# A global-filter FFT block with a SwiGLU feed-forward on one core: the transforms one unit later, output stores in four places, the first filter piece after the rows, turned rows kept by lanes

## The chip, the core and the metric

The kernel runs on one core of a Trainium2 chip. The core has a matrix engine (TensorE, "PE" in the profile, with its weight loads as "PEld"), VectorE ("DVE"), ScalarE ("ACT"), GpSimd ("POOL") and SyncE ("SP", which here only issues transfers). Each engine works through its own instructions in their order; engines wait for one another by semaphores. Sixteen DMA engines carry the transfers. The metric is the device time of one execution in microseconds (us), the median of several runs.

## What is computed

The input is x, 8 batches of 3008 tokens with 256 channels. Along the tokens a real FFT is taken, multiplied by a complex filter, and transformed back. Every one of the 24,064 resulting rows then goes through a gated feed-forward with 1536 hidden units. All in 32-bit floats.

```python
def _attn_ref(x, filt_r, filt_i):
    X = np.fft.rfft(x, axis=1)
    F = (filt_r + 1j * filt_i)[None, :, :]
    y = np.fft.irfft(X * F, n=x.shape[1], axis=1)
    return y.astype(np.float32)

def _moe_ref(x, w_gate, w_val, w_out):
    g = x @ w_gate
    silu = g * (1.0 / (1.0 + np.exp(-g)))
    val = x @ w_val
    return (silu * val @ w_out).astype(np.float32)
```

## The kernel before

**Units.** The rows after the transform lie in `y_t`, channels on partitions, and are worked on in 47 stripes of 512 rows. A stripe has 12 units, one for each 128 hidden units; there are 564 units, and the loop at the end of the kernel runs over them. Its turn n holds the gate and value products of unit n (`products`, L925 and L929, results ws and wx), their evaluation on ScalarE and VectorE (L247, L952, L951, L954, result h), the split of h of unit n-1 into two parts of fewer bits and their sum (`split_high`, `split_low`: hh, hl, hs; the latter two on GpSimd, L241), and the product of unit n-2 with the output weights (`project`, L979 to L982, two halves c). The first 24 units (stripes 0 and 1) are "plain": they use whole-precision weights (L915, L974) while the split weights are still being made. After the last unit of a stripe the sums are taken out of the accumulators (`evacuate`: turn n with n % 12 == 1, two ScalarE and two VectorE instructions), transposed on VectorE in the next turn (`turn_out`, L1001), and stored in the one after (`store`, four quarters q, one transfer each, or more pieces in batch 0).

**Places in a turn.** A turn has places for other work, "a", "b", "c", "p" and "z": "a" at its start, "b" between gate and value, "c" before the projections, "p" between the two halves of the projection. Work for a place is entered with `at(n, place, f)` or, for a generator that runs up to its next `yield` at each place, with `steps`. This fixes the order on each engine's queue.

**Weights.** Six of the twelve weight pieces stay on the chip, six are fetched anew for each stripe, always two units ahead in that list: at "a" of every other turn SP issues a piece of the gate and value weights (gv, 768 KB) and one of the output weights (wo, 384 KB), L1064. Each waits for the last product that read its place.

**Transforms.** 3008 is 47 x 64. Batch 0 is transformed ahead of the loop. For each later batch b, the transform is spread over the turns while earlier rows go through the feed-forward, counted from u0 = 60 + 72 (b - 2), or 0 for b = 1. Its steps:
- `turn_rows` (four parts, at u0 - 24, -22, -20, -18; for b = 1 all at turn 0) copies rows of x in reverse order, from DRAM to a DRAM buffer `turned`; `load_x(g)` reads a group of them and the straight rows into `lent`, `fold(g)` makes sums and differences on VectorE (four instructions, two in each of two turns).
- `quads(g)`, g = 0 to 3: two bursts of products (L619), copies and sums (the VectorE copy is L636, the last sums are on GpSimd), four stores to `quads_dram`. After g = 3, `load_four(0)` reads them back, turned round.
- `there(w)`, w = 0 to 5: a burst (L713), then the product with the filter (`load_filter(w)`, 1 MB) on VectorE and GpSimd, for which one half is exchanged by an SBUF to SBUF transfer (lent<-raw); its last sum is on VectorE (L238).
- `home(w)`, five turns after there(w): a burst (L688), a copy on ScalarE, two sums on VectorE, two stores to `d2`.
- `load_t4(k)` and `back(k, m)`: eight bursts (L772), each with two transposes on VectorE into `y_t` (L778).

The numbers `q_at`, `there_at`, `home_at`, `back_at`, `first_fold` are the turns of these steps. For b > 1 quads begin at u0 + 1, 5, 9, 13, there at 20, 26, ... 50, home at 25, ... 55, back at 60, 61, 63 to 68. `split_y` splits the next stripe of `y_t` into parts, at places listed in `free`, `later` and `after`. The buffer `lent` is shared by all of it (`room_of`); its x rows, the filter piece and t4 lie in the same place. Products rotate over four accumulator banks; a burst takes the two that come next.

**SP's queue.** All of these transfers, the weights' and the output's too, are issued by SP in the order in which the places come. If one has to wait, those behind it wait too. Only weight loads of the first stage go by GpSimd's queue.

Of the kernel before, what the change touches and what calls it, by code (L numbers as in the profile page):

```python
# [129 lines left out]
def kernel(  # L130
# [62 lines left out]

    dram_tiles = [wdpool.tile([2 * NS, N2, C], FP32, name=f"d2_{i}") for i in range(2)]
    quads_dram = [wdpool.tile([64, N2, C], FP32, name=f"quads_{i}") for i in range(2)]
    turned_dram = [wdpool.tile([16, 128, C], FP32, name=f"turned_{i}") for i in range(2)]
    gv_dram = wdpool.tile([ND, 128, 2, 2, 3, 128], F32R, name="gv_all")
    wo_dram = wdpool.tile([ND, 128, 2, 3, 128], F32R, name="wo_all")
    f_dram = wdpool.tile([128, 2, NS, C], FP32, name="filter")
# [221 lines left out]
    class Spectral:  # L421
# [146 lines left out]
        def turn_rows(self, part):  # L568

            xb, to = x[self.b], self.turned  # L570
            end = NS if self.b > 2 else 32
            h, lane, n = part // 2, 32 * part, 16 * part
            p = 1 - h
            self.load(out=to[:, lane + p:lane + end],
                      in_=bass.AP(tensor=xb.tensor, ap=[[C, 16], [-N2 * C, end - p], [1, C]],
                                  offset=xb.offset + ((N1 - 1) * N2 + n) * C))
            if h == 0:
                self.load(out=to[:, lane], in_=xb[n:n + 16])

        def load_x(self, u):  # L580
            if u < N_QUAD // 2:
                self.x[u] = [room_of("x", n) for n in range(2)]
                up, down = self.x[u]
                at = self.turned.rearrange("(g q) p c -> g p q c", q=4)[u]
                self.load(out=down.rearrange("p (q c) -> p q c", c=C), in_=at)
                rows = x[self.b].rearrange("(r n) c -> r n c", n=N2)
                for n in range(4):
                    first = 16 * n + 4 * u
                    self.load(out=up[ts(n, 32)].rearrange("p (q c) -> p q c", c=C),
                              in_=rows[0:32, first:first + 4])  # L590
# [14 lines left out]
        def quads(self, g):  # L605

            pieces = (g, g + N_QUAD // 2)
            parts = self.x.pop(g)
            t1 = {u: room_of("yg"[i]).rearrange("p (n h c) -> p n h c", h=2, c=C)
                  for i, u in enumerate(pieces)}  # L610
            views = {}

            def burst(h):
                banks = {u: bank(f"qa_{self.b}_{u}_{h}") for u in pieces}
                for cp in range(2):
                    for t in range(2):
                        for i, u in enumerate(pieces):
                            r, c = 32 * (2 * h + i), 32 * (2 * cp + t)
                            pin(nc.tensor.matmul(  # L619
                                out=banks[u][c:c + 32], lhsT=quad_t[r:r + NS, ts(t, 32)],  # L620
                                rhs=parts[t][r:r + NS, ts(cp, NV * C)],
                                start=True, stop=True))
                for u, t in banks.items():
                    views[u, h] = t.rearrange("p (n c) -> p n c", c=C)

            d1 = self.quads_dram.rearrange("a (n h) c -> a n (h c)", h=2)
            v, e, act = nc.vector, nc.gpsimd, nc.scalar
            a, b = pieces
            burst(0)
            if g == 3:  # L630
                self.load_filter(0)
                self.load_turns(0)
            yield
            pin(act.copy(out=t1[a][:, :, 0], in_=views[a, 0]))
            yield
            pin(v.tensor_copy(out=t1[b][:, :, 0], in_=views[b, 0]))  # L636
            yield
            burst(1)
            yield
            m = t1pool.tile([128, 2 * NV, C], FP32, name=f"raw_{self.b}_{g}", tag="t1", bufs=1)[:, 0:NV]  # L640
            pin(act.copy(out=m, in_=views[b, 1]))
            yield
            pin(sub(v, t1[a][:, :, 1], t1[a][:, :, 0], views[a, 1]))
            pin(add(v, t1[a][:, :, 0], t1[a][:, :, 0], views[a, 1]))
            yield
            pin(sub(e, t1[b][:, :, 1], t1[b][:, :, 0], m))
            yield
            pin(add(e, t1[b][:, :, 0], t1[b][:, :, 0], m))
            yield
            for u in pieces:  # L650
                for cp in range(2):
                    n = 4 * u + 2 * cp
                    self.load(out=d1[:, n:n + 2], in_=t1[u][64 * cp:64 * cp + 64])
            if g == 3:
                self.load_four(0)

        def load_four(self, w):

# [344 lines left out]
    def store(u):  # L1003
        o, j = evacuated[u.j].rearrange("p i z c -> p i (z c)"), u.j

        def rows(q, t0, t1, i0, i1, token, step):
            pin(nc.sync.dma_start(
                out=bass.AP(tensor=out.tensor, offset=out.offset + token * C + 64 * q,
                            ap=[[step * C, t1 - t0], [32 * step * C, i1 - i0], [1, 64]]),
                in_=o[32 * q + t0:32 * q + t1, i0:i1]))  # L1010

        end = min(max(S - T * j, 0), T)
        pieces = []
        for k in range(NCHUNK):
            a, b = max(T * j, NK0 * k), min(T * j + end, NK0 * (k + 1))
            while a < b:
                i, t0 = divmod(a - T * j, 32)
                full = (b - a) // 32
                if t0 or not full:
                    n, t1 = 1, min(32, t0 + b - a)  # L1020
                else:
                    n, t1 = full, 32
                pieces.append((t0, t1, i, i + n, 4 * (a - NK0 * k) + k, 4))
                a += (t1 - t0) if n == 1 else 32 * n
        if end < T:
            pieces.append((0, 32, end // 32, 16, T * j + end, 1))
        for q in range(4):
            for piece in pieces:
                rows(q, *piece)


    units_of = []
# [12 lines left out]
    def at(n, place, f, *args):  # L1045
        hooks.setdefault((n, place), []).append((f, args))
# [6 lines left out]
    def lazily(make):  # L1053

        def piece():
            yield from make()

        return piece()
# [49 lines left out]
    for b in range(1, B):  # L1108
        s = specs[b]
        if b == 1:  # L1110
            u0, q_at, there_at = 0, [5, 8, 11, 14], [18, 22, 27, 32, 37, 42]
            home_at = [m + 4 for m in there_at]
            back_at, first_fold = range(51, 59), [(4, "a"), (4, "b"), (4, "c"), (5, "a")]
        else:
            u0 = 60 + BATCH * (b - 2)
            q_at, there_at = [1, 5, 9, 13], [20 + 6 * w for w in range(N_FOUR)]
            home_at = [m + 5 for m in there_at]
            back_at = (60, 61, 63, 64, 65, 66, 67, 68)
            first_fold = [(-1, "b"), (-1, "c"), (0, "a"), (0, "b")]
            for part in range(4):  # L1120
                at(u0 - 24 + 2 * part, "c", s.turn_rows, part)
            at(u0 - (3 if b == 2 else 7), "c" if b == 2 else "a", s.load_x, 0)
        at_u0 = lambda places: [(u0 + m, p) for m, p in places]
        fold = lambda g, s=s: lazily(lambda: s.fold(g))
        steps(fold(0), at_u0(first_fold))
# [14 lines left out]
        for k, n, place in ((1, home_at[-1] + 2, "c"), (0, home_at[-1] + 3, "b"), (2, home_at[-1] + 3, "c"),  # L1140
                            (3, back_at[1] + 1, "a")):
            at(u0 + n, place, s.load_t4, k)
        for n, (k, m) in zip(back_at, ((1, 0), (1, 1), (0, 0), (0, 1), (2, 0), (3, 0), (2, 1), (3, 1))):
            n += u0
            steps(lazily(lambda s=s, k=k, m=m: s.back(k, m)), [(n, "p"), (n + 1, "a"), (n + 1, "a")])

# [4 lines left out]
    for j in range(PLAIN, NSTRIPE):  # L1151
# [3 lines left out]
        m = (n - 60) % BATCH or BATCH  # L1155
        free = {24: "17b 17b 17c 18b 18c 18c 19b 19c", 36: "22b 22b 22c 23b 28b 28b 28c 31b",
                48: "36b 36b 36c 37b 40b 40b 41b 42b", 60: "48b 48b 48c 49b 50b 50b 50c 51b"}.get(n)
        later = {12: "0b 1b 1c 2b 3b 4b 5b 6b", 24: "15b 16b 17b 18b 17b 18b 19b 20b",
                 36: "24b 24b 25b 26b 28b 29b 31b 32b", 48: "36b 36b 37b 38b 40b 41b 43b 44b",
                 60: "48b 48b 49b 50b 52b 53b 55b 56b", 72: "60b 60b 60c 61b 62b 62b 62c 63b"}[m]  # L1160
        after = "67b 67b 67c 68b 68b 68b 69b 70b" if n > 60 else "57b 57b 57c 58b 58b 58b 58c 59b"

        def places_of(text, base):
# [25 lines left out]
    def projections(n, u):  # L1189
        if u:  # L1190
            u.project(0)
            if u.last:
                evacuate(u, 0)
        run_hooks(n, "p")
        if u:
            u.project(1)
            if u.last:
                evacuate(u, 1)
                end = n + 1 if n < NU else n
                for c in range(2):  # L1200
                    at(end, "c", turn_out, u, c)
                at(end + 1, "a", store, u)
        run_hooks(n, "z")

    for n in range(NU + 2):
# [23 lines left out]
        if n != N_PLAIN + 1:  # L1229
            projections(n, two_back)  # L1230
        if n == NU + 1:
            for m in (n, n + 1, n + 2):
                for place in "abcp":
                    run_hooks(m, place)
    assert not hooks, sorted(hooks)
# [28 lines left out]
```

## Time and profile before

| | |
|---|---|
| runs | 2769.06, 2769.44, 2774.63 us; median 2769.44 |
| profiled execution | 2778.99 us, of which 2777.2 are the span from the first to the last instruction |
| TensorE's granted clock | 0.994 of full speed on average |
| instructions | 44,446 |
| DMA | 598.16 MB, 215 GB/s, 311,118 packets |
| first non-plain product | 224 us |
| batches 2 to 7, six periods of 72 units | 399.5 to 2468.1 us: 349.1, 344.3, 342.5, 342.2, 343.0, 347.4 |
| after that, feed-forward alone | to the end |

A matrix product of 128 x 512 is shown with some 390 ns, but products overlap: in an undisturbed stretch one begins every 0.227 us. So a nearly always busy TensorE can still be slowed, and the time of a turn says more than the busy share. The groups of the page: line, engine, operation, result<-operands, form, count, then busy us and mean ns of one, then the idle time of the engine before them and what ended it.

```profile
L929 PE MATMUL wx<-yh,gv 128*128 128x512 f32 x2160 | 850.2, 394 | 23.4 <-DVE lent L238 11.5
L925 PE MATMUL ws<-ys,gv 128*128 128x512 f32 x2160 | 673.2, 393 | 24.4 <-DMA gv<-gv_all 15.8
L954 DVE TENSOR_TENSOR h<-wx,g 128x512 f32<-128x512 f32 x540 | 373.7, 692 | 72.3 <-DVE wx L247 2.4
L241 POOL TENSOR_TENSOR hs<-hh,hl 128x512 fp32r<-128x512 f32 x540 | 717.4, 1329 | 42.3
```

### The profile page before, as it was taken

Reading aid. Unit: us, or ns where it says so; the run is one execution under the profiler, and the core shown is the slowest. Engines: PE = TensorE matmul, PEld = TensorE weight load, DVE = VectorE, ACT = ScalarE, POOL = GpSimd, SP = SyncE. Lnnn points to the kernel's source line nnn. Section 1 sums busy time; section 2 is a strip of 40 time slices with the busy share of each in tenths; the row PEclk is TensorE's granted clock in tenths of the full one; section 3 lists DMA queues with packets and bytes.
Section 4 is the critical chain, followed back from the end, with each engine's and each line's share of the span. In section 5 each row is a group of like instructions: output and inputs, shape, how many; then the busy total and the mean of one; then the engine's idle time right before and its main releaser. Section 6 shows DMA issues by size and latency. Waiting matters only on the chain.

```text
span 2777.2 us, 44446 instructions
## 1 busy us (share of the span) xinstructions
PE 2698.5 (97%) x14476; PEld 2005.1 (72%) x14476; DVE 1844.4 (66%) x2600; ACT 1821.0 (66%) x3433; POOL 1980.0 (71%) x1613
## 2 busy tenths in 40 slices
PE   8999999999999999999999999999999999999998
PEld 6446776777767776677777777777777677778886
DVE  5885677566785667756677666776667756665554
ACT  5555665676666666677666666666666667666775
POOL 3675766787677776787767777677866777777775
PEclk9999999999999999999999999999999999999999
DMA  9967777778577785777857778577785777744443
GB/s 232 315 198 222 253 200 225 218 245 237 179 229 225 246 242 164 232 239 240 245 169 224 235 246 241 169 238 237 235 243 159 229 225 238 230 137 154 159 154 106
DMA packets 311118, 598.16 MB, mean 215 GB/s; under 512 B 124378, under 2 KB 181624, under 8 KB 310424
## 3 DMA queue, kind: packets, MB, share of 16 engines
q1 hardware_dynamic: 308136, 587.33, 69.0%
q0 software_dynamic: 2608, 7.93, 1.0%
q8 instruction: 116, 1.90, 0.3%
q14 instruction: 114, 0.93, 0.1%
q10 hardware_dynamic: 144, 0.07, 0.0%
HBM read 486.56 MB, written 104.60 MB: 213 GB/s over the span
## 4 chain that ended last, share of the span: by engine, by line
PE 72%; DMA 7%; DVE 7%; POOL 6%; ACT 3%; issue 3%; SPq 1%; DVEq 0%; POOLq 0%; ACTq 0%
PE wx L929 28%; PE ws L925 14%; PE o L979 8%; PE o L980 7%; PE o L982 7%; PE wpd L772 2%; POOL hs L241 2%; DMA gv<-gv_all 2%; POOL hl L241 2%; PE wqc L688 2%; DVE lent L241 1%; PE wqb L713 1%; DMA lent<-raw 1%; PE wqa L619 1%; DMA quads<-lent 1%
## 5 line engine op out<-in xcount | busy, mean ns | idle before, releaser
L241 POOL TENSOR_TENSOR hl<-h,hs 128x512 fp32r<-128x512 f32 x540 | 698.8, 1294 | 609.3 <-ACT hs L244 568.0
L929 PE MATMUL wx<-yh,gv 128*128 128x512 f32 x2160 | 850.2, 394 | 23.4 <-DVE lent L238 11.5
L929 PE MATMUL wx<-yl,gv 128*128 128x512 f32 x2160 | 843.5, 391 | 0.0
L241 POOL TENSOR_TENSOR hs<-hh,hl 128x512 fp32r<-128x512 f32 x540 | 717.4, 1329 | 42.3
L244 ACT ACTIVATE hh<-h 128x512 fp32r<-128x512 f32 x540 | 341.7, 633 | 551.8 <-DVE h L954 479.9
L925 PE MATMUL ws<-ys,gv 128*128 128x512 f32 x2160 | 673.2, 393 | 24.4 <-DMA gv<-gv_all 15.8
L247 DVE SCALAR_TENSOR_TENSOR g<-wx,g 128x512 f32<-128x512 f32 x540 | 372.2, 689 | 376.0 <-ACT g L244 304.6
L247 DVE SCALAR_TENSOR_TENSOR wx<-wx,v 128x512 f32<-128x512 f32 x540 | 377.2, 698 | 322.7 <-PE wx L929 185.7
L929 PEld LDWEIGHTS wx<-yh,gv 128*128 128x128 f32 x2160 | 406.7, 188 | 136.5 <-PE ws L925 26.5
L925 PEld LDWEIGHTS ws<-ys,gv 128*128 128x128 f32 x2160 | 405.1, 189 | 121.5 <-PE wx L929 15.2
L929 PEld LDWEIGHTS wx<-yl,gv 128*128 128x128 f32 x2160 | 406.7, 188 | 83.2
L979 PE MATMUL o<-hs,wo 128*128 128x512 f32 x1080 | 443.7, 411 | 8.3 <-POOL hs L241 8.1
L980 PE MATMUL o<-hh,wo 128*128 128x512 f32 x1080 | 422.7, 391 | 0.0
L982 PE MATMUL o<-hl,wo 128*128 128x512 f32 x1080 | 421.7, 390 | 0.0
L954 DVE TENSOR_TENSOR h<-wx,g 128x512 f32<-128x512 f32 x540 | 373.7, 692 | 72.3 <-DVE wx L247 2.4
L244 ACT ACTIVATE g<-ws 128x512 f32<-128x512 f32 x540 | 317.5, 588 | 71.8 <-PE ws L925 69.2
L952 ACT ACTIVATE g<-g 128x512 f32<-128x512 f32 x540 | 343.8, 637 | 12.6 <-DVE g L247 12.0
L951 ACT COPY v<-ws 128x512 f32<-128x512 f32 x540 | 314.7, 583 | 38.2 <-PE ws L925 34.9
L244 ACT ACTIVATE hs<-h 128x512 fp32r<-128x512 f32 x540 | 337.2, 624 | 0.0
L979 PEld LDWEIGHTS o<-hs,wo 128*128 128x128 f32 x1080 | 202.7, 188 | 145.8 <-issue 95.3
L982 PEld LDWEIGHTS o<-hl,wo 128*128 128x128 f32 x1080 | 203.2, 188 | 43.5
L980 PEld LDWEIGHTS o<-hh,wo 128*128 128x128 f32 x1080 | 203.4, 188 | 34.7
(113 smaller groups left out, 2415.4 us busy)
## 6 DMA issues: line engine op xcount, KB each, us to landing
gv<-gv_all SPq DMA_DIRECT2D x268, 768.0 KB
wo<-wo_all SPq DMA_DIRECT2D x268, 384.0 KB
lent<-filter SPq DMA_DIRECT2D x42, 1024.0 KB
quads<-lent SPq DMA_DIRECT2D x112, 256.0 KB
out_dram<-o SPq DMA_DIRECT2D x172, 128.0 KB
lent<-quads SPq DMA_DIRECT2D x168, 128.0 KB
lent<-raw SPq DMA_DIRECT2D x84, 256.0 KB
d<-lent SPq DMA_DIRECT2D x84, 256.0 KB
```

Of the source, the lines that this page charges most:

```text
L241: return eng.tensor_tensor(out=dst, in0=a, in1=b, op=ALU.subtract)
L244: return nc.scalar.activation(out=dst, in_=a, func=AF.Copy, scale=scale)
L247: return nc.vector.scalar_tensor_tensor(out=dst, in0=a, scalar=scale, in1=b, op0=ALU.mult, op1=op)
L688: pin(nc.tensor.matmul(out=home[e][s // 2 * 64:s // 2 * 64 + 64, s % 2 * C:s % 2 * C + C], lhsT=tb[r, 1, 64 * s:64 * s + 64], rhs=y[r, s], ...
L925: pin(nc.tensor.matmul(out=s, lhsT=w[:, a, 2], rhs=yb[:, a], start=a == 0, stop=a == 1, skip_group_check=True))
L929: pin(nc.tensor.matmul(out=p, lhsT=w[:, a, n], rhs=t[:, a], start=a + n == 0, stop=a + n == 2, skip_group_check=True))
L951: pin(nc.scalar.copy(out=v, in_=s))
L952: pin(nc.scalar.activation(out=self.g, in_=self.g, func=AF.Silu))
L954: pin(nc.vector.tensor_tensor(out=self.h, in0=p, in1=self.g, op=ALU.mult))
L979: pin(nc.tensor.matmul(out=s, lhsT=w[:, c, 2], rhs=both, stop=self.last, **kw))
L980: pin(nc.tensor.matmul(out=p, lhsT=w[:, c, 0], rhs=hi, stop=False, **kw))
L982: pin(nc.tensor.matmul(out=p, lhsT=w[:, c, 1], rhs=lo, stop=self.last, **kw))
```

## The change

- For batches 2 to 7 quads, there, home and back begin one unit later or up to two (back is now at 62 to 69 without a gap, in another order of its parts, also for batch 1), and the first fold with them; load_x(0) moves from u0 - 7 to u0 - 4 for batches 3 to 7. The places of `split_y` in `later` move too. `turn_rows` stays where it was.
- `store` yields after each quarter, so that the transfers of a stripe are issued at four places of two turns.
- `load_filter(0)` is issued after `load_four(0)` instead of at the first burst of quads(3).
- `turned` is laid out as [128 lanes, 16 rows, channels] instead of [16, 128, channels]. `load_x` reads 4 KB in one piece for each lane. `turn_rows` writes, as its outermost dimension, two groups of 8 rows, each 8 KB in one piece, for 23 to 32 lanes; before it wrote 16 rows, each 1 KB, for as many lanes.

```diff
--- before.py
+++ after.py
@@ -193,7 +193,7 @@
 
     dram_tiles = [wdpool.tile([2 * NS, N2, C], FP32, name=f"d2_{i}") for i in range(2)]
     quads_dram = [wdpool.tile([64, N2, C], FP32, name=f"quads_{i}") for i in range(2)]
-    turned_dram = [wdpool.tile([16, 128, C], FP32, name=f"turned_{i}") for i in range(2)]
+    turned_dram = [wdpool.tile([128, 16, C], FP32, name=f"turned_{i}") for i in range(2)]
     gv_dram = wdpool.tile([ND, 128, 2, 2, 3, 128], F32R, name="gv_all")
     wo_dram = wdpool.tile([ND, 128, 2, 3, 128], F32R, name="wo_all")
     f_dram = wdpool.tile([128, 2, NS, C], FP32, name="filter")
@@ -571,18 +571,17 @@
             end = NS if self.b > 2 else 32
             h, lane, n = part // 2, 32 * part, 16 * part
             p = 1 - h
-            self.load(out=to[:, lane + p:lane + end],
-                      in_=bass.AP(tensor=xb.tensor, ap=[[C, 16], [-N2 * C, end - p], [1, C]],
+            self.load(out=to[lane + p:lane + end].rearrange("p (a n) c -> a p (n c)", a=2),
+                      in_=bass.AP(tensor=xb.tensor, ap=[[8 * C, 2], [-N2 * C, end - p], [1, 8 * C]],
                                   offset=xb.offset + ((N1 - 1) * N2 + n) * C))
             if h == 0:
-                self.load(out=to[:, lane], in_=xb[n:n + 16])
+                self.load(out=to[lane], in_=xb[n:n + 16])
 
         def load_x(self, u):
             if u < N_QUAD // 2:
                 self.x[u] = [room_of("x", n) for n in range(2)]
                 up, down = self.x[u]
-                at = self.turned.rearrange("(g q) p c -> g p q c", q=4)[u]
-                self.load(out=down.rearrange("p (q c) -> p q c", c=C), in_=at)
+                self.load(out=down.rearrange("p (q c) -> p q c", c=C), in_=self.turned[:, ts(u, 4)])
                 rows = x[self.b].rearrange("(r n) c -> r n c", n=N2)
                 for n in range(4):
                     first = 16 * n + 4 * u
@@ -628,7 +627,6 @@
             a, b = pieces
             burst(0)
             if g == 3:
-                self.load_filter(0)
                 self.load_turns(0)
             yield
             pin(act.copy(out=t1[a][:, :, 0], in_=views[a, 0]))
@@ -653,6 +651,7 @@
                     self.load(out=d1[:, n:n + 2], in_=t1[u][64 * cp:64 * cp + 64])
             if g == 3:
                 self.load_four(0)
+                self.load_filter(0)
 
         def load_four(self, w):
 
@@ -1027,6 +1026,7 @@
         for q in range(4):
             for piece in pieces:
                 rows(q, *piece)
+            yield
 
 
     units_of = []
@@ -1113,13 +1113,13 @@
             back_at, first_fold = range(51, 59), [(4, "a"), (4, "b"), (4, "c"), (5, "a")]
         else:
             u0 = 60 + BATCH * (b - 2)
-            q_at, there_at = [1, 5, 9, 13], [20 + 6 * w for w in range(N_FOUR)]
+            q_at, there_at = [2, 6, 10, 14], [21 + 6 * w for w in range(N_FOUR)]
             home_at = [m + 5 for m in there_at]
-            back_at = (60, 61, 63, 64, 65, 66, 67, 68)
-            first_fold = [(-1, "b"), (-1, "c"), (0, "a"), (0, "b")]
+            back_at = range(62, 70)
+            first_fold = [(0, "b"), (0, "c"), (1, "a"), (1, "b")]
             for part in range(4):
                 at(u0 - 24 + 2 * part, "c", s.turn_rows, part)
-            at(u0 - (3 if b == 2 else 7), "c" if b == 2 else "a", s.load_x, 0)
+            at(u0 - (3 if b == 2 else 4), "c" if b == 2 else "a", s.load_x, 0)
         at_u0 = lambda places: [(u0 + m, p) for m, p in places]
         fold = lambda g, s=s: lazily(lambda: s.fold(g))
         steps(fold(0), at_u0(first_fold))
@@ -1140,7 +1140,7 @@
         for k, n, place in ((1, home_at[-1] + 2, "c"), (0, home_at[-1] + 3, "b"), (2, home_at[-1] + 3, "c"),
                             (3, back_at[1] + 1, "a")):
             at(u0 + n, place, s.load_t4, k)
-        for n, (k, m) in zip(back_at, ((1, 0), (1, 1), (0, 0), (0, 1), (2, 0), (3, 0), (2, 1), (3, 1))):
+        for n, (k, m) in zip(back_at, ((1, 0), (1, 1), (0, 0), (2, 0), (3, 0), (0, 1), (2, 1), (3, 1))):
             n += u0
             steps(lazily(lambda s=s, k=k, m=m: s.back(k, m)), [(n, "p"), (n + 1, "a"), (n + 1, "a")])
 
@@ -1155,9 +1155,9 @@
         m = (n - 60) % BATCH or BATCH
         free = {24: "17b 17b 17c 18b 18c 18c 19b 19c", 36: "22b 22b 22c 23b 28b 28b 28c 31b",
                 48: "36b 36b 36c 37b 40b 40b 41b 42b", 60: "48b 48b 48c 49b 50b 50b 50c 51b"}.get(n)
-        later = {12: "0b 1b 1c 2b 3b 4b 5b 6b", 24: "15b 16b 17b 18b 17b 18b 19b 20b",
-                 36: "24b 24b 25b 26b 28b 29b 31b 32b", 48: "36b 36b 37b 38b 40b 41b 43b 44b",
-                 60: "48b 48b 49b 50b 52b 53b 55b 56b", 72: "60b 60b 60c 61b 62b 62b 62c 63b"}[m]
+        later = {12: "0b 0b 1b 2b 4b 5b 6b 7b", 24: "12b 12b 14b 15b 16b 17b 18b 19b",
+                 36: "24b 24b 26b 27b 29b 30b 32b 33b", 48: "36b 36b 38b 39b 41b 42b 44b 45b",
+                 60: "48b 48b 50b 51b 53b 54b 56b 57b", 72: "60b 60b 60c 61b 62b 62b 62c 63b"}[m]
         after = "67b 67b 67c 68b 68b 68b 69b 70b" if n > 60 else "57b 57b 57c 58b 58b 58b 58c 59b"
 
         def places_of(text, base):
@@ -1199,7 +1199,7 @@
                 end = n + 1 if n < NU else n
                 for c in range(2):
                     at(end, "c", turn_out, u, c)
-                at(end + 1, "a", store, u)
+                steps(lazily(lambda: store(u)), [(end + 1, "a"), (end + 1, "c"), (end + 2, "a"), (end + 2, "c")])
         run_hooks(n, "z")
 
     for n in range(NU + 2):
@@ -1229,7 +1229,7 @@
         if n != N_PLAIN + 1:
             projections(n, two_back)
         if n == NU + 1:
-            for m in (n, n + 1, n + 2):
+            for m in range(n, n + 4):
                 for place in "abcp":
                     run_hooks(m, place)
     assert not hooks, sorted(hooks)
```

## The prediction

> **What bounds the kernel now.** I read the page first, then TensorE's waits, then its instructions in order of time, unit by unit, then SP's queue and the DMA records.
>
> ```profile
> PE 2698.5 (97%) x14476; PEld 2005.1 (72%) x14476; DVE 1844.4 (66%) x2600; ACT 1821.0 (66%) x3433; POOL 1980.0 (71%) x1613
> ```
>
> TensorE is never idle for long: 78.7 of 2777.2 us. Its waits, by what ended them:
>
> ```profile
> PE ws L925 <- DMA gv<-gv_all: 15.8, 6, 5.1
> PE wx L929 <- DVE lent L238: 11.5, 19, 0.6
> PE o L979 <- POOL hs L241: 8.1, 8, 2.3
> PE wx L929 <- DVE lent L636: 6.3, 10, 1.9
> ```
>
> (us in total, times, longest.) None is large; what they cost is read from slots. I call "slot n" the stretch from the first L925 product of unit n to that of unit n+1, and +m the slot u0+m of a batch. Undisturbed, a slot is 4.08 us (18 products, 0.227 us from one to the next); with a burst of there, home or back 5.33, with half a quads 5.5. The six periods of 72 slots of batches 2 to 7 take 2068.5 us. Undisturbed, one would take 72 x 4.08 for the products, 20 bursts x 1.25 and 8 halves of quads x 1.43: 330.5, six 1983. So 85 us at most can be won there, and every transfer that comes late can lose more.
>
> The DMA engines are the second resource:
>
> ```profile
> 284.00:332.00 48.00, 46.71 (x247) 35.34 (x246) 31.47 (x45) 34.58 (x65) 39.09 (x31) 1.00 0.86 289
> 635.00:671.00 36.00, 33.72 (x179) 25.48 (x177) 24.07 (x34) 25.02 (x47) 26.76 (x21) 1.00 0.80 255
> 2500.00:2550.00 50.00, 50.00 (x222) 41.40 (x221) 27.73 (x41) 35.16 (x66) 33.63 (x27) 1.00 0.47 162
> ```
>
> (Window; busy us of PE, PEld, DVE, ACT, POOL; granted clock, DMA share, GB/s.) In the stretches where the next batch's rows are turned, the sixteen are busy 80 to 86% of the time; beside the plain feed-forward of the end 47%.
>
> **The change, part by part.** Sums are made against the profiled execution (2778.99 us, span 2777.2), which is 9.5 over the median 2769.44; I put the difference on the median.
>
> *One slot later.* (1) At +20 TensorE waits for gv: slots +19 and +20 last 13.59, 14.00, 11.46, 11.60, 11.52 and 16.05 us in batches 2 to 7 instead of 4.08 + 5.33, in all 21.8 too long (with the half clock that follows three of the waits). SP issued that gv, due at slot 17 "a", only at +18, because the quads stores and `load_four(0)` at 16 "c" stand before it and wait for GpSimd's sum and for the stores' landing. One slot later they stand behind it, and the next gv has until +22: it follows 0.5 MB of quads rows (16 packets x 0.121 us per engine, 2.5 as they came here), 1 MB of filter (16 x 0.159) and 0.4 MB of wo (8 x 0.121), takes 8 x 0.234 itself, in all 8 us from the landing of the quads stores at about 19 + 1.6, and has 2 to 3 us to spare. I take -21.8 (bounds -21.8 and 0). (2) At +26, +38 and +50 home meets the stripe's evacuation: 6.20 instead of 5.33 us, 15.7 us in all. After, home meets the two transposes (L1001, 0.69 each), and the sum of `there` on VectorE (L238, 1.44) now stands ahead of the evacuation. VectorE's order becomes h(25), that sum, two evacuations (0.69 each), g(26), wx(26), h(26), two transposes, home's two sums. Laid out by these durations, g(26) ends at 3.8 in slot 26, where the burst wants its bank at 3.5: 0.35; home's second sum ends at 2.1 in slot 27, where the next wx wants its bank at 1.8: 0.45 with the semaphore. Together 0.80. I take -1 (bounds -15.7, +6). (3) back at +61 with the evacuation makes +62 1.38 too long; at +62 it meets the transposes instead, and my layout gives 0.97: -2.5 (bounds -8.3, 0). (4) New: fold(3) ends at 13 "c", in front of the evacuation. Its last half (1.5) and the two evacuations (1.37) precede g(14), whose bank the quads burst needs: slot +14 about 2.1 too long, where +13 to +15 were 1.2 before. +5 for six (bounds 0, +9). (5) raw leaves SP in an even slot, away from gv, wo and the output: up to -6 (slots +54, +55), but the rows below stand there, so 0. (6) The rest that moves: `load_x(0)` three slots later still has four slots (17 us; its 1 MB landed some 8 us after its issue at 1745); `load_t4(3)` at +64 lands within 6 us, as from 1726.9, and back(3,0) uses it at +66, 14 us on; the splits of y move with the transforms, with the same count of instructions on ScalarE and GpSimd: 0 (a late one costs what its wait lasts).
>
> *Stores one by one.* In batch 2 stripe 5 has sixteen pieces; they hold SP from 416.7 to 426.3, the quads store comes late, VectorE's L636 too, and +6 lasts 9.29 instead of 5.52: -3.8 (bounds -3.8, 0). Elsewhere the same issues stand in four places; nothing else waits for them.
>
> *Filter piece behind the rows.* 16 packets of 4 KB by 0.159 us per engine, first read at +22: hidden by there(0) and the slots +19 to +21, 0 (2.5 us a batch if the slack above is gone). It passes the four quads stores, `load_four(0)` and the wo and gv of slots 15 and 17, which now leave without it.
>
> *Turned rows by lanes.* Reading them changes from 32 packets of 1 KB (46 ns) per engine to 8 of 4 KB (159): -0.2 us each, hidden. Writing them is what I expect to decide. Before, such a store is [16] x [23 to 32] pieces of 1 KB: 23 x 46 ns = 1.07 us (1.46 for 31 or 32 rows), on all sixteen engines. After, it is [2] x [23 to 32] pieces of 8 KB. Do two rows spread over sixteen engines?
>
> ```profile
> wf_t<-wf_tbl SPq DMA_DIRECT2D x1, 47.0 KB
> turned<-in_x_dram SPq DMA_DIRECT2D x10, 384.0 KB
> turned<-in_x_dram SPq DMA_DIRECT2D x10, 368.0 KB
> ```
>
> The trace has a transfer that tells: wf_t is 94 rows of 512 B, and its packets start in pairs, 47 pairs, from 1.67 to 3.05 us, 27 ns each: two engines at work. The completion writes agree: a transfer on sixteen engines leaves sixteen packets of 4 bytes, 1697 transfers of SP would leave 27,152, and there are 27,034. With 2 engines for the 94 rows, 14 for each of eight transfers of 14 rows and 4 for each of six of 4 rows, 102 of the 118 missing are explained (16 are one transfer's). So the number of engines follows the outermost count, and for 2 rows I take two engines. The Trainium skill, "DMA: Bandwidth & Descriptors", section "Why a DMA increments its semaphore by 16 and not by 1", says the same: as many engines, up to 16, as divide the slowest dimension of both sides; by it the sum stands. Its "Specifications" put an engine at about 27 GiB/s, by which the 38.9 us below would be an estimated 36.
>
> The price of 8 KB on one engine: the fastest such packets of the trace took 0.309 us, and 24 KB from DRAM to DRAM 0.912, the same rate. So 7.1 to 7.4 us a store (23, 24 rows), 9.6 to 9.9 (31, 32), on two engines in whose queues all later transfers of SP have a share.
>
> Batch 1: four stores at once.
>
> ```profile
> 70.85 3.94 SPq L438 DMA_DIRECT2D turned<-in_x_dram  x6
> 82.45 0.37 SPq L438 DMA_DIRECT2D lent<-turned  x1
> 95.12 0.69 DVE L238 TENSOR_TENSOR lent<-lent 128x512 f32<-128x512 f32 x1
> ```
>
> Here SP waits 6.2 us for them, and fold(0) starts at 95.1. After: 126 packets x 0.309 = 38.9 us from about 73.5, and seven weight loads of GpSimd's queue share the engines (16 x 46 ns or 8 x 121, 0.85 each): 118. Then `load_x(0)`, 6.5 us as now: 125. fold(0) waits for it, every VectorE instruction behind it too (h of the plain units, the weights' rounding), and TensorE stops: +30 (bounds +20, +38).
>
> Batch 2 (rows stored at units 36 to 42, 284 to 332 us): an engine is busy 0.86 x 48 = 41.3 us, less 4 x 1.46 of the old stores 35.5, plus 39.0: 74.5 in 48. Batches 3 to 7 (slots +48 to +54): 0.80 x 36 = 28.8, less 4.3, plus 29.0: 53.5 in 36. Too much by 26.5 and 17.5; the last gv of the window has some 10 us to spare (issued 666.7, needed 680.1, 2.9 for itself and wo). So 16.5 once, and 7.5 five times; with the clock halved afterwards (3.41 us, as after the waits of 503 and 2223: 1.7) and SP held up, since it uses eight completion semaphores and so has eight transfers under way at most, 10 each. +66.5 (bounds: slack covers all, 0; no slack, +28 and 5 x 19 = +123).
>
> **Sum:** -21.8 - 1 - 2.5 + 5 - 3.8 = -24.1; +30 + 16.5 + 50 = +96.5. Together +72.4, so 2769.4 + 72.4 = **2842**.
>
> **Rivals.** *Sixteen engines after all:* the store is cut up so that it spreads. For it: contiguous rows of 24 KB were cut into sixteen. Against: the 94 rows were left. Then -24.1 and the -6 of (5): **2739**, faster. It decides if turned's landing in batch 1 stays near 82 us. *Two engines, but later batches have the slack:* the rows are needed only 14 slots on, and each gv is asked for three slots ahead. Then +30 - 30: **2769**. Against: the window sums above. *No slack at all:* +38, +28, +95 less 24: **2907**; for it, gv is one of several transfers that have to come through the same two queues (raw holds GpSimd, which holds hs).
>
> **How the numbers follow.** Two engines with loss as summed 66%, sixteen engines 16%, slack 8%, no slack 10%. The likeliest gives 2842. Its bounds alone are 2790 to 2905; 2755 to 2905 leaves out the sixteen engines and the upper end. About 0.2% (5.5 us) is what can be told from no change: faster 17% (sixteen engines, a little of the slack case), same 5%, slower 78%.
>
> **What would show it.** Right: SP's wait for turned in batch 1 of 30 us or more, VectorE idle before fold(0) ended by lent's loads, TensorE waiting for gv or hs in slots +54 to +58 of batches 2 to 6 and not 7; the gv wait at +20 gone; L636 at +6 of batch 2 gone; +14 near 7.6 us; +26 to +27 still 0.8 too long together. Wrong: turned landing after some 10 us, DMA share unchanged in slots +48 to +58, and the time under the old one.

## The result and the profile after

The changed kernel takes 2841.9 us (median of four runs, 2836.4 to 2848.8) against 2769.7 before: 1.0252 times as long, 95% interval 1.0233 to 1.0271. The profiled execution took 2848.8 us with a span of 2847.0, that of before 2777.2.

Where the time lies, from the first gate product of one unit to that of another (us):

| stretch | before | after | difference |
|---|---|---|---|
| start to unit 24 (batch 1's rows) | 224.0 | 258.8 | +34.8 |
| units 24 to 59 (batch 2's rows) | 175.5 | 201.1 | +25.6 |
| six periods of batches 2 to 7 | 2068.5 | 2079.4 | +10.9 |
| the rest | 309.2 | 307.7 | -1.5 |

The six periods are 348.6, 348.8, 348.3, 347.4, 348.2 and 338.0. The last one, in which no further batch is turned, is 9.4 us faster than before; the second to fifth are some 5 us slower.

The page, busy time and TensorE's clock in 40 slices:

```profile
PE 2719.4 (96%) x14476; PEld 2018.8 (71%) x14476; DVE 1840.8 (65%) x2600; ACT 1824.4 (64%) x3433; POOL 1989.2 (70%) x1613
...
PE   8699889999999998999999999999989999999998
...
PEclk9799989999999999999999999999999999999999
```

The second slice (71 to 142 us) is the one with a hole, and there the granted clock falls too. TensorE's waits of the changed kernel (us in total, times, longest):

```profile
PE ws L924 <- DMA gv<-gv_all: 51.8, 12, 6.8
PE wqa L618 <- ACT g L936: 26.1, 1, 26.1
...
PE o L978 <- POOL hs L241: 7.0, 6, 2.4
...
PE wx L928 <- DVE lent L238: 3.2, 16, 0.5
```

The wait for gv has grown from 15.8 to 51.8 us, and one wait of 26.1 is new. The old gv waits at +20 are nearly gone; the new ones end at unit 42 (6.5 us), 44 (5.8), 46 (4.4) and at +56 of batches 2 to 6 (6.1, 6.7, 6.8, 6.3, 6.2), none in batch 7. The waits for lent (L238 at home, L636 at quads) have shrunk or gone.

**Batch 1.** SP's queue in order of time, start and duration of each group of issues:

```profile
75.36 3.75 SPq L438 DMA_DIRECT2D turned<-in_x_dram  x6
79.48 19.84 SPq L460 DMA_DIRECT2D t<-d  x1
122.07 0.34 SPq L438 DMA_DIRECT2D lent<-turned  x1
```

and VectorE's, with the idle time before and its releaser:

```profile
130.22 0.69 DVE L238 TENSOR_TENSOR lent<-lent 128x512 f32<-128x512 f32 x1 [32.64 <-DMA lent<-in_x_dram]
```

The turned rows are read 46.7 us after their first store was issued; before it was 11.6. VectorE stands 32.6 us in front of fold(0), with everything that is queued behind it. What the DMA engines do in that time is seen in the windows (busy us and instructions of PE, PEld, DVE, ACT and POOL, granted clock, DMA share, GB/s), first of the changed kernel, then of the one before while its turned stores ran:

```profile
105.00:121.00 16.00, 2.74 (x7) 0.95 (x5) 0.00 (x0) 0.00 (x0) 0.00 (x0) 0.73 0.13 54
```

```profile
70.00:82.00 12.00, 12.00 (x35) 6.94 (x34) 8.55 (x24) 3.47 (x8) 4.54 (x8) 0.72 0.91 292
```

A share of 0.13 of sixteen engines is two engines; they move 54 GB/s, 27 each, and in the packet records 8 KB packets run two at a time. The other fourteen are idle. The completion writes, one of 4 bytes from each engine that took part, say the same: the page of the kernel before counts 124,378 packets under 512 B, that of the changed one 123,986. That is 392 fewer, 14 for each of the 28 two-group stores. The Trainium skill's rule ("DMA: Bandwidth & Descriptors", "Why a DMA increments its semaphore by 16 and not by 1") gives two engines for an outermost dimension of 2; the trace agrees.

**Later batches.** SP's queue in batch 3, about slots +51 to +54, of the changed kernel:

```profile
1049.99 3.65 SPq L438 DMA_DIRECT2D d<-lent  x2
1053.69 5.07 SPq L1006 DMA_DIRECT2D out_dram<-o  x2
1058.88 3.86 SPq L438 DMA_DIRECT2D lent<-raw  x2
1062.84 0.54 SPq L438 DMA_DIRECT2D lent<-four_tbl  x1
1063.42 0.71 SPq L438 DMA_DIRECT2D turned<-in_x_dram  x1
1064.18 0.48 SPq L1006 DMA_DIRECT2D out_dram<-o  x1
1064.76 0.43 SPq L1064 DMA_DIRECT2D wo<-wo_all  x1
1065.23 0.74 SPq L1064 DMA_DIRECT2D gv<-gv_all  x1
```

and the same stretch of the first experiment below, which differs only in that these stores use sixteen engines:

```profile
980.16 1.32 SPq L438 DMA_DIRECT2D d<-lent  x2
981.54 2.30 SPq L1006 DMA_DIRECT2D out_dram<-o  x2
984.54 1.39 SPq L438 DMA_DIRECT2D lent<-raw  x2
986.03 0.53 SPq L438 DMA_DIRECT2D lent<-four_tbl  x1
986.61 0.61 SPq L438 DMA_DIRECT2D turned<-in_x_dram  x1
987.26 0.61 SPq L1006 DMA_DIRECT2D out_dram<-o  x1
988.18 0.35 SPq L1064 DMA_DIRECT2D wo<-wo_all  x1
988.58 0.46 SPq L1064 DMA_DIRECT2D gv<-gv_all  x1
```

From d to gv it is 8.4 us there and 15.2 here. In the trace SP's transfers use eight completion semaphores in turn, and each one waits until the one eight places back has landed. The third store of the output, at 1058.45, stood 2.9 us until a turned store had landed; besides, the issues themselves last longer (d 3.65 us for 1.32, raw 3.86 for 1.39), and the traces do not show why. So gv leaves 7.4 us after the start of its slot (+53, at 1057.8) instead of 0.6 (988.0). Then it needs 12.5 us to land instead of 7.0, and TensorE waits 6.7 us for it at 1077.86. With sixteen engines there were 11.6 us from issue to use and no wait.

The delay at SP and the delay between issue and landing are about equal: on average of the five batches gv leaves 6.6 us after the start of the slot instead of 0.9, and needs 12.8 us to land instead of 6.5. Its completion writes show where the second is lost. In each of the five, fourteen of the sixteen have come 5.2 to 6.8 us after the issue, the last two only after 12.2 to 13.1. In batch 3, 112 of gv's 128 packets start by 1071.5, but the turned store issued just before it keeps its engines busy with 8 KB packets until 1073.9, and the other sixteen, the share of two engines, come after that.

### The profile page after: what moved, and what is told of

It reads as the page before. It is cut to its first block, busy times and chain, and to the rows that moved or that the text cites. A ratio compares the mean times of both kernels' runs of the same rounds, so it can differ in the third digit from the quotient of the medians.

```text
span 2847.0 us, 44523 instructions
## 1 busy us (share of the span) xinstructions
PE 2719.4 (96%) x14476; PEld 2018.8 (71%) x14476; DVE 1840.8 (65%) x2600; ACT 1824.4 (64%) x3433; POOL 1989.2 (70%) x1613
## 4 chain that ended last, share of the span: by engine, by line
PE 75%; DMA 12%; DVE 7%; ACT 2%; issue 1%; POOL 1%; SPq 1%; DVEq 0%; POOLq 0%; ACTq 0%
PE wx L928 30%; PE ws L924 15%; PE o L978 8%; PE o L979 7%; PE o L981 7%; DMA gv<-gv_all 4%; DMA turned<-in_x_dram 2%; PE wqa L618 2%; DVE lent L241 2%; PE wpd L771 2%; PE wqc L687 2%; PE wqb L712 1%; DVE o L1000 1%; DMA lent<-raw 1%; DVE h L953 1%
## 5 line engine op out<-in xcount | busy, mean ns | idle before, releaser
L928 PE MATMUL wx<-yh,gv 128*128 128x512 f32 x2160 | 853.4, 395 | 11.6 <-DVE h L953 6.7
L924 PE MATMUL ws<-ys,gv 128*128 128x512 f32 x2160 | 678.1, 395 | 55.8 <-DMA gv<-gv_all 51.8
L978 PEld LDWEIGHTS o<-hs,wo 128*128 128x128 f32 x1080 | 202.6, 188 | 141.2 <-issue 94.7
```

The source lines that it names most:

```text
L924: pin(nc.tensor.matmul(out=s, lhsT=w[:, a, 2], rhs=yb[:, a], start=a == 0, stop=a == 1, skip_group_check=True))
L928: pin(nc.tensor.matmul(out=p, lhsT=w[:, a, n], rhs=t[:, a], start=a + n == 0, stop=a + n == 2, skip_group_check=True))
L978: pin(nc.tensor.matmul(out=s, lhsT=w[:, c, 2], rhs=both, stop=self.last, **kw))
```

## The experiments

In each, what is not in the diff is as in the kernel named. The kernel before was run again beside each group of them, with medians from 2769.4 to 2774.0 us; each ratio below is against its own group's.

**Sixteen engines for the stores, layout by lanes kept** (changed kernel with):

```diff
-            self.load(out=to[lane + p:lane + end].rearrange("p (a n) c -> a p (n c)", a=2),
-                      in_=bass.AP(tensor=xb.tensor, ap=[[8 * C, 2], [-N2 * C, end - p], [1, 8 * C]],
+            self.load(out=to[lane + p:lane + end].rearrange("p (a n) c -> a p (n c)", a=16),
+                      in_=bass.AP(tensor=xb.tensor, ap=[[1 * C, 16], [-N2 * C, end - p], [1, 1 * C]],
```

> The changed kernel with one thing other: turned keeps its layout by lanes, but its stores have 16 rows of 1 KB as the outermost dimension instead of 2 groups of 8 KB. Theory (two engines for two groups are the loss): the waits for gv at units 42 to 46 and at slots +55 of batches 2 to 6 go, fold(0) starts near 95 us again, and the time is that of my sixteen-engine case, 2739 (2733 to 2746). Rival (the layout by lanes or the moved stores are the loss, whatever the engines): it stays above 2800.

2737.3 us (2736.5 to 2739.0), 0.988 of before [0.9864, 0.9897]. TensorE's waits now:

```profile
PE wx L928 <- DVE h L953: 6.6, 24, 0.5
...
PE ws L924 <- DMA gv<-gv_all: 1.6, 1, 1.6
```

and the first instruction of fold(0):

```profile
97.75 0.69 DVE L238 TENSOR_TENSOR lent<-lent 128x512 f32<-128x512 f32 x1 [4.16 <-DMA lent<-in_x_dram]
```

One gv wait is left of twelve, and fold(0) starts at 97.75 instead of 130.22. The outermost dimension of one transfer is worth 105 us, and with sixteen rows there the change is a gain of 1.2%. Lanes and moved stores are not the loss.

**Four and eight groups** (the same two lines with 4 groups of 4 KB, and with 8 of 2 KB).

> The changed kernel with the turned stores as 4 groups of 4 KB. Theory (capacity of so many engines, with slack): in batch 1 the rows land 17 us later than before (39.6 later with 2 groups, times (1/4 - 1/16) / (1/2 - 1/16)); some 5 us of that were covered, so +12; in the later windows four engines have 55 us of work in 48 and 39 in 36, which the slack of 10 covers: 2739 + 12 = 2751 (2747 to 2762). Rival (loss in proportion to the engines' extra time, no slack): 100 x 0.43 = 43, so 2782.

> The changed kernel with the turned stores as 8 groups of 2 KB. Theory (eight engines, capacity with slack): batch 1's rows land 6 us later than with 16, which costs 1; in the windows eight engines have 45 us of work in 48 and 32 in 36: nothing. 2738 (2735 to 2742). Rival (in proportion to the engines' extra time): 100 x (1/8 - 1/16) / (1/2 - 1/16) = 14 more, 2751.

Four: 2758.1 (2756.8 to 2759.6), 0.9955 [0.994, 0.997]. Eight: 2745.7 (2742.2 to 2746.1), 0.9895 [0.9878, 0.9911]. From the first turned store to the reading of the rows it is 14.3 us with 16 groups, 18.8 with 8, 28.6 with 4, 46.7 with 2; from that store to unit 24 it is 155.7, 158.8, 165.3 and 183.5. So rows that are 4.5, 14.3 and 32.4 us later cost 3.1, 9.6 and 27.8: 1.4 of the short delay is covered and some 5 of the long ones, as reckoned for those. Eight came out 3.7 us above my range; in its profiled execution (2746.1) 3.1 us are lost up to unit 24, where I had 1, and 2.8 more because the first store was issued later (at 74.2 instead of 71.4; it was 70.4 to 75.4 in all these profiles). Four lost another 10.3 in units 24 to 59, where I expected nothing: waits for gv at unit 44 and for hs at 46, 3.5 us each, after SP had stood 4.1 and 3.5 us until a turned store landed, and half clock behind both. The proportional rival is refuted for four (2782) and eight (2751); the six periods are as short with four (2028.5) and eight (2029.9) as with sixteen (2028.0).

Length of a piece and number of engines change together in these four versions, so their times alone don't tell the two apart. The pages do: against sixteen rows, the completion writes are 224 fewer with eight groups (28 x 8), 336 with four (28 x 12) and 392 with two (28 x 14), as many as engines that take no part. And the two engines move 27 GB/s each: 1 KB in 46 ns is 22, so the long piece in itself is not what is slow.

**Turned as before the change, the rest changed** (layout, stores and read undone).

```diff
-            self.load(out=to[lane + p:lane + end].rearrange("p (a n) c -> a p (n c)", a=2),
+            self.load(out=to[:, lane + p:lane + end],
...
-                self.load(out=down.rearrange("p (q c) -> p q c", c=C), in_=self.turned[:, ts(u, 4)])
+                at = self.turned.rearrange("(g q) p c -> g p q c", q=4)[u]
+                self.load(out=down.rearrange("p (q c) -> p q c", c=C), in_=at)
```

> The changed kernel with turned laid out, stored and read as before the change. Theory (the loss is the stores' engine count, the layout is worth nothing): the same as with 16 rows of 1 KB by lanes within 4 us, 2739 (2733 to 2746). Rival (reading 4 KB pieces is worth something): some us slower than that.

2739.1 (2737.4 to 2746.5), 0.9891 [0.9874, 0.9909]: no difference from the first experiment. Reading 4 KB pieces instead of 1 KB is worth nothing that can be measured here.

**Turned by lanes in two groups alone, in the kernel before** (the diff's first three hunks only).

> The kernel before with nothing but the new turned layout and its stores in two groups. Theory (the parts of the change add up): 2770 + 100 = 2870 (2855 to 2885), with the gv waits near +54 and at +20 both there. Rival (the loss comes from the stores meeting the moved transforms): below 2840.

2871.2 (2869.7 to 2872.8), 1.0363 [1.0348, 1.0379]. Its rows are 46.9 us from store to read, units 24 to 59 take 204.4, and its first five periods 350.5 to 352.8. Both losses of slots are there: +53 to +59 are 9.1 to 10.6 us too long in five batches, and +19 and +20 still 14.6 in six (21.8 in the kernel before). The loss does not need the moved transforms. It is 100.3 us here and 104.6 beside them, so the parts add up within 5 us.

**Two groups for batch 1 alone.**

```diff
-            self.load(out=to[lane + p:lane + end].rearrange("p (a n) c -> a p (n c)", a=2),
-                      in_=bass.AP(tensor=xb.tensor, ap=[[8 * C, 2], [-N2 * C, end - p], [1, 8 * C]],
+            a = 2 if self.b == 1 else 16
+            m = 16 // a
+            self.load(out=to[lane + p:lane + end].rearrange("p (a n) c -> a p (n c)", a=a),
+                      in_=bass.AP(tensor=xb.tensor, ap=[[m * C, a], [-N2 * C, end - p], [1, m * C]],
```

> The changed kernel with two groups of 8 KB for batch 1 alone and 16 rows of 1 KB for batches 2 to 7. Theory (the 28 us that units 24 to 60 lose come from batch 2's stores at units 36 to 42): 2737 + 32 = 2769 (2763 to 2776), units 24 to 60 again in some 173 us. Rival (they are an after-effect of batch 1's late start): 2797.

2767.0 (2763.7 to 2769.7), 0.997 [0.9957, 0.9984]. Unit 24 at 255.3, units 24 to 59 in 173.5, the periods as with sixteen. The rival falls: what units 24 to 59 lose comes from batch 2's own stores.

**The two-group stores from another engine's queue.** First ScalarE for all of them, then GpSimd for batches 2 to 7:

```diff
+        def turn_load(self, **kw):
+            pin(nc.scalar.dma_start(**kw))
...
-            self.load(out=to[lane + p:lane + end].rearrange("p (a n) c -> a p (n c)", a=2),
+            self.turn_load(out=to[lane + p:lane + end].rearrange("p (a n) c -> a p (n c)", a=2),
```

> The changed kernel, stores of turned in two groups as it has them, but issued by ScalarE on its own queue instead of SP's. Theory (a gv comes late since SP's own transfers stand behind 8 KB packets in the queues of two engines, and since SP stands at a semaphore until turned has landed): both go, a gv's packets now alternate with turned's on two engines, 8 x (0.234 + 0.309) = 4.3 us, which its lead covers; the waits at +55 (46.7 us in five batches against the 16-row stores) and in units 24 to 60 (28.0) go, batch 1's 31.7 stay, since the rows themselves are late: 2842 - 75 = 2767 (2757 to 2785). Rival (two engines' capacity decides, on whatever queue): above 2820.

2860.1 (2854.2 to 2861.1), 1.0322 [1.0305, 1.0339]: slower still. The time lies where the rival said, above 2820, but neither theory nor rival had the cause. ScalarE's instructions in batch 3, with idle time and releaser, and its waits over the whole execution:

```profile
1069.55 0.64 ACT L954 ACTIVATE g<-g 128x512 f32<-128x512 f32 x1
1073.04 0.59 ACTq L443 DMA_DIRECT2D turned<-in_x_dram  x1
1073.74 0.63 ACT L244 ACTIVATE hh<-h 128x512 fp32r<-128x512 f32 x1 [3.54 <-DMA turned<-in_x_dram]
```

```profile
ACT hh L244 <- DMA wo<-wo_all: 22.0, 2, 19.8
ACT hh L244 <- DMA turned<-in_x_dram: 21.4, 5, 4.9
```

ScalarE's issue at 1073.04 stood until an earlier turned store had landed, and once 19.8 us until wo, a transfer of SP, had. The trace names the semaphores: in this program ScalarE's transfers use the same eight completion semaphores as SP's. So the hold moved to an engine that TensorE needs in every slot. Of the theory, the part about gv's own way holds: the gv of slot +53 lands 8.4 us after its issue, on average of the five batches, instead of 12.8. But SP issued it 11.1 us after the start of the slot instead of 6.6; SP, too, still stood until turned stores had landed.

> The changed kernel, with the two-group stores of batches 2 to 7 issued by GpSimd on its own queue; batch 1's stay with SP. With ScalarE as issuer the wait moved to ScalarE: its issues stood until a transfer of SP, or an earlier turned store, had landed. Theory (the wait for a free completion semaphore is the larger part, two shared engines the smaller): GpSimd has semaphores of its own; units 24 to 60 lose 10 instead of 28, slots +53 to +59 of batches 2 to 6 some 3 each instead of 9.3: 2842 - 18 - 31 = 2793 (2770 to 2815). Rival (capacity of the two engines alone): 2842, above 2820. Rival (the semaphores alone): 2767.

2807.2 (2803.7 to 2811.4), 1.0121 [1.0105, 1.0138]; units 24 to 59 in 184.1 (expected 183), slots +53 to +59 too long by 6.1, 4.2, 6.5, 5.2 and 5.9 (expected 3 each). TensorE's waits for gv, 51.8 us in the changed kernel, and for hs are now:

```profile
PE ws L927 <- DMA gv<-gv_all: 14.1, 6, 4.7
PE o L981 <- POOL hs L241: 14.1, 7, 4.0
```

GpSimd's transfers use eight other semaphores in the trace. Some 36 of the 75 us that were lost behind batch 1 are gone (17.0 in units 24 to 59, 18.9 in the five batches). The gv of slot +53 leaves 4.4 us after the start of the slot on average instead of 6.6, and needs 11.8 us to land instead of 12.8: more is won at SP than behind the issue. How much of it is the semaphores alone can't be told, since the stores were also spread over more engines: where two of them overlap, four of their 8 KB packets run at once (11 us in all of batches 2 to 7), where with SP's queue it was three at most (3.4 us). Most of the time it is two, as before (149 of 209 us). The section of the Trainium skill named above says that transfers of GpSimd's queue start at a moving engine and those of SP at the lowest; that agrees. The size of each part stays open.

**The other parts, one by one.** Version with sixteen engines and all output stores at once again; the same with the first filter piece at its old place; and the kernel before with the shift alone:

```diff
-                steps(lazily(lambda: store(u)), [(end + 1, "a"), (end + 1, "c"), (end + 2, "a"), (end + 2, "c")])
+                at(end + 1, "a", store, u)
```

> The version with 16-row stores, its output stores all at once again as before the change. Theory: slots +5 to +7 of batch 2 get back the 4.8 us that they lost less: 2742 (2740 to 2745), in the trace L636 late at +6 or +7 of batch 2. Rival (one slot later the quads store no longer stands behind the sixteen pieces): 2737, no difference.

2739.7 (2737.0 to 2744.9), 0.9888 [0.987, 0.9906], slots +5 to +7 of batch 2 in 15.65 us as with separate stores (15.61; 20.41 before the change). The rival holds: one slot later the quads stores no longer stand behind the sixteen pieces, and issuing one by one is worth nothing that can be measured.

```diff
             if g == 3:
+                self.load_filter(0)
                 self.load_turns(0)
...
                 self.load_four(0)
-                self.load_filter(0)
```

> The version with 16-row stores, the first filter piece asked for at the first burst of quads(3) again, as before the change. Theory of the prediction (its place is worth nothing): 2737 +- 3, slots +21 and +22 together within 0.5 us a batch of 9.6. Rival (there it holds the quads stores up, as SP waits for its room): 2.5 us a batch, 2752. Rival (behind the rows it stands in front of the gv of slot +20): faster by the 2.5 us that +21 and +22 are now too long in all batches together, 2734.

2734.7 (2733.8 to 2736.5), 0.9869 [0.9854, 0.9884]. The traces tell more than the times: slots +17 to +23 of the six batches take 178.8 instead of 181.7, the seven slots undisturbed but for one burst (29.81) in each batch. In its new place the filter piece stands in front of the gv of +20; the third reading was right about that. But it is not the whole: with the old place slots +0 to +16 take 1.9 us longer, so the six periods together gain only 0.9 (2027.1 against 2028.0). Of the 2.9 us between the two profiled executions 2.3 lie ahead of unit 24, which comes anywhere from 223.9 to 230.1 in the kernels that keep sixteen engines.

> The kernel before with the transforms one slot later and nothing else: old stores, old filter place, old turned. Theory: the shift is the gain and the stores in four places give 4.8 on top: 2739 + 5 = 2744 (2740 to 2750). Rival (shift, stores and filter place need each other, the gv of slot +20 being late again without them): 2757 or more.

2735.7 (2733.7 to 2747.3), 0.988 [0.9856, 0.9905]. The shift, with the folds, `load_x(0)`, the order of back and the splits that move with it, gives the whole gain alone. The 4.8 us that the theory added for stores all at once are not lost, so it comes out under its range, and the rival falls.

**There and home two slots later** (kernel before with the shift alone, and):

```diff
-            q_at, there_at = [2, 6, 10, 14], [21 + 6 * w for w in range(N_FOUR)]
+            q_at, there_at = [2, 6, 10, 14], [22 + 6 * w for w in range(N_FOUR)]
```

> The kernel before with the shift alone, but there and home two slots later than before (there at 22, 28, .. 52, home at 27, .. 57), quads and back one later. It tests the terms (2) and (5). Theory: home is now clear of the evacuation (25, 37, 49) and of the transposes (26, 38, 50), so the 0.45 + 0.45 us of slots +26 and +27, +38 and +39, +50 and +51 go: 18 x 0.9 = 16 less; raw leaves SP in an odd slot as before the change, beside gv and wo, and the 7 us of slots +53 to +59 come back: 2736 - 16 + 7 = 2727 (2719 to 2736). Rival (the parity of raw's slot is not what mattered): 2720. Rival (home one slot later makes t4 late for back): back's slots longer, above 2736.

2731.3 (2727.1 to 2735.1), 0.986 [0.9838, 0.9882], the fastest of all, though not clear of the version above. Home's slots give back 10.1 us, not 16: 5.56 is left where 5.33 would be undisturbed. Raw's waits come back in part, but earlier, at +44 and +45 (slots +43 to +47: 137.4 to 141.2), not at +54. GpSimd's wait for raw in the kernel before, with the shift alone, and here:

```profile
POOL lent L745 <- DMA lent<-raw: 33.1, 16, 8.6
```

```profile
POOL lent L745 <- DMA lent<-raw: 9.3, 2, 8.6
```

```profile
POOL lent L745 <- DMA lent<-raw: 20.4, 9, 8.6
```

So the slot in which raw leaves matters, but it alone does not explain the 7 us at +54.

## Why the prediction was right

The time came out as forecast (2842 against 2841.9), and by the mechanism forecast. That the two agree to the microsecond is luck: the gain was larger than summed (some 33 us instead of 24.1), and so was the loss (105 instead of 96.5).

| term | predicted | measured |
|---|---|---|
| (1) gv at +20 | -21.8 | -21.9 with the shift alone, -19.0 with the filter piece moved too, -16.0 in the changed kernel |
| (2) home, slots +25 to +29, +37 to +41, +49 to +52 | -1 | -0.4 |
| (3) back | -2.5 | -2.7 |
| (4) quads, without batch 2's +5 to +7 | +5 | -3.7 (-0.7 with the shift alone) |
| stores one by one (batch 2) | -3.8 | -4.8 is gained, but by the shift |
| (5) slots +53 to +59 | 0 (to -6) | -7.0 |
| batch 1's rows | +30 | +30.3 from the first store to unit 24; it was issued 4.5 later |
| batch 2's rows, units 24 to 59 | +16.5 | +28.0 against sixteen engines |
| rows of batches 3 to 7, slots +53 to +59 | +50 | +46.7 against sixteen engines |

The gains are those of the first experiment against before, unless named otherwise.

The decisive step, two engines for two rows, is shown by the first experiment, by the 54 GB/s, by the completion writes, by the two engines on which gv is late, and by the last period, which has no turned rows and no loss. Of the signs, SP's queue has two waits instead of one: 19.8 us for a result of GpSimd, and then 22.5 for turned, under the 30 that I gave as a sign for the latter. VectorE's wait for lent's loads, the waits of batches 2 to 6 and not 7, L636 and slot +14 (7.3 to 7.6) came as said; +26 and +27 together are 0.9 too long, where 0.8 was said. Of gv at +20, 5.9 us in six batches is left at +21 and +22.

What was mis-sized: *batch 2's rows* (16.5 for 28.0). The 16.5 was the waiting alone, and TensorE does wait 16.7 us there for gv. What the sum left out is what comes with it: the clock is halved for 6.83 us at 351 and at 368 and for 3.41 at 385 and at 392, of which 14.6 us are not waiting; work then goes at half speed, so 7.3 are lost, and the waits for hs are 3.0. For the later batches the prediction had counted the half clock, for this one not.

*Rows of batches 3 to 7* (10 a batch for 9.3). The size is right, but its parts were not. The sum took the gv issued at 666.7, with 10 us to spare; the one that comes late is the one before it, issued at 659.7, which had 5.0 (4.4 to 6.6 in the five batches). And SP's lateness, for which less than 1 us a batch was left, is 5.7 against sixteen engines. That these parts make up the sum is luck too. The run with four groups shows the limit of such a sum over a window: by capacity nothing, measured 10.3, since SP stood at single landings and each wait drew half clock after it.

*Quads* (+5 for -3.7): I laid out +14 alone, which is 7.3 to 7.7 us, as said; that the first quads, at +1 to +3, would get 1.1 us a batch faster away from the evacuation, I did not lay out. *(5)*: that raw comes earlier was seen, but I took nothing for it, since the turned rows stand there; on sixteen engines they do no harm.

The rivals: sixteen engines would have given 2739, and the kernel made so gives 2737. Slack covering the later batches is refuted by units 24 to 59 and the five periods, no slack at all by the 46.7 us there, half of its 95. Two figures of the prediction do not come out of its own terms: "no slack at all" adds up to 2906, not 2907, and no sum there gives the bounds 2790 and 2905.

## What to carry to other kernels

The outermost dimension of a transfer set how many DMA engines carried it here (2, 4, 8 or 16); making pieces longer by folding rows into them can take engines away, and 8 KB pieces on two engines cost 105 us here against 1 KB pieces on sixteen. Look at a large transfer's DMA share in a window, not only at its bytes. A slow transfer harms more than its readers: every other transfer with a share on its engines is late, and the issuer stands when it comes round to a semaphore whose transfer has not landed. A sum of capacity over a window does not see that, and another engine's queue is no cure if it draws on the same semaphores. Try a change of several parts one by one: here one part held all of the gain and another all of the loss.

## What the runs showed that was not expected

- ScalarE's transfers wait for the landing of SP's and of each other: 22.0 and 21.4 us of ScalarE's time in the run that issued from there.
- Of a gv's sixteen engines two are late by some 7 us behind a two-group store, and the whole transfer lands with them; SP issues it 5.7 us later besides.
- The same two-group stores issued by GpSimd run four 8 KB packets at once where two stores overlap, those of SP two.
- Longer pieces did not pay on reading either: 8 packets of 4 KB per engine against 32 of 1 KB made no difference to the time (2737.3 against 2739.1).
